# Agent attention and maxout layer on one core: a side path's transfers on GpSimd's queue, 72 transfers instead of 74, agents loaded as 28 partitions

## The chip, the cores and the metric

The kernel runs on one core of a Trainium2 chip. The metric is device time in microseconds (us), the median of several runs. Two kernels that differ by less than about 0.2% cannot be told apart by it. One execution was also recorded by the hardware profiler; the span of its page runs from the first to the last instruction.

## The reference

With B = 4, N = 12544, C = 128, 49 agent rows per batch and d_ff = 768:

```python
sm = softmax(scale * a @ b.T)
agent_v = sm(agents, k) @ v            # [4, 49, 128]
x = (sm(q, agents) @ agent_v)          # [4, 12544, 128]
h = max(x @ w1, x @ w2, x @ w3)        # [50176, 768]
out = h @ w_out                        # [50176, 128], float32
```

q, k and v are float32 and 25.7 MB each; the output is as large.

## The kernel before

The keys are worked in 56 groups of seven tiles of 128 rows (operations `kc`, `kt`, `ke`, `ks`, `kx`, `vc`, `kv`), the queries in 49 groups of eight tiles (`qc` to `ov`); group 48 takes the two tiles left over of each batch. Each output row is a mixture of the 49 rows of `agent_v`, and the kernel folds the maxout layer into small tables `G` per batch, so that a query group needs few products. That folding has room for CAPACITY = 64 hidden units that are undecided; whether the room is enough is computed on the chip (`c0`, `c1`, `good`, `worst`), read into a register on every engine (line 274), and tested by a branch (line 275). When the test fails, `in_general` (lines 635 to 737) computes everything again without the folding. With the given inputs the test holds and the branch skips it.

The graph of operations is built in `graph`, and the string ORDER lists all of them in the order in which they are emitted; each engine runs its own in that order. Operands wait in numbered slots (`SLOTS`): LD has five slots for loaded float32 groups, OS five for outputs, QT three for transposed queries.

All the large transfers are issued by SyncE (SP), in ORDER's order: 32 loads of k and v (`kl`, `vl`, line 302), four weights (line 349), 17 loads of q (`ql`, line 553) and 20 stores (`st`, line 561). A store waits for the scaling operations `ov` (line 628 on VectorE; for the second half of group 47 line 631 on ScalarE) that fill its part of an OS slot. Stores up to group 44 take three query groups, 24 tiles, 12 KB per partition. The last groups go alone: 45 and 46 as eight tiles each, 47 in two halves of four tiles, and 48, whose store stands ahead of group 44's.

The agents are the one transfer outside SP in the part that runs: ScalarE's queue issues it first of all (line 217), as 49 partitions of four rows, one row per batch, into the tile `sums_of`. `prep` (lines 287 to 296) casts them to bf16, transposes them batch by batch on TensorE, and copies each of the four results to `agT`, which the scores of the keys need.

The landing of each transfer is told by a semaphore. There are eight of these for the transfers of SP and ScalarE together, taken in turn in the order of the program, so the ninth transfer uses the first one's again. The skipped path's own transfers (lines 652, 668, 704, 737) are on ScalarE's queue in this kernel, and so belong to the same eight. Because the skipped path would have moved these semaphores, an engine that skips it has to bring them to the values that the path would have left: these are the semaphore instructions that the profile puts at line 275. The instructions at line 870 end the program: SP waits for all semaphores, two in an instruction, the transfers' eight in their order, and then the engines meet.

Of the kernel before, what the change touches and what calls it, by code (L numbers as in the profile page):

```python
# [24 lines left out]
VC = C + 2  # L25
CAPACITY = 64
LEAST, MOST = 1e-15, 1e15
KEYS, EARLY = B * A, WHOLE * 3 + 6
TG, TK = 3, 4
LONG = TG * GT  # L30

PE, ACT, DVE, POOL, SP = range(5)
# [77 lines left out]
def graph(plan, em):  # L110
# [52 lines left out]
    for s in range(NQ):  # L163
        parts = parts_of(s)
        np_ = len(parts)
        gx, gy = [f"gx{p[0]}" for p in parts], [f"gy{p[0]}" for p in parts]
        z = s // TG * TG
        if s == z:
            add(f"ql.{s}", SP, em.q_load(s), new=[("LD", f"q.{s}")], **dma(524 if s == NQ - 1 else TG * 524))
        add(f"qc.{s}", POOL, em.q_cast(s), (0.98, 1.1), after=[f"ql.{z}"], new=[("QB", f"qb.{s}")], use=[f"q.{z}"])  # L170
        add(f"qt.{s}", PE, em.q_turn(s), mm(GT, 128), after=[f"qc.{s}", "prep"], new=[("M", f"qT_ps.{s}")], use=[f"qb.{s}"])
        add(f"qe.{s}", ACT, em.q_evacuate(s), act(1024), after=[f"qt.{s}"], new=[("QT", f"qT.{s}")], use=[f"qT_ps.{s}"])
        add(f"sc.{s}", PE, em.q_scores(s), mm(2 * np_, 512 // np_), after=[f"qe.{s}"], new=[("M", f"qs.{s}")], use=[f"qT.{s}"])
        add(f"ex.{s}", ACT, em.q_exps(s), (0.478, 0.655), after=[f"sc.{s}"], new=[("EQ", f"e.{s}")], use=[f"qs.{s}"])
        add(f"su.{s}", PE, em.sums(s), mm(GT // 2, 2), after=[f"ex.{s}"], use=[f"e.{s}", f"qs.{s}"])
        add(f"re.{s}", DVE, em.recips(s), (0.118, 0.3), after=[f"su.{s}"], use=[f"qs.{s}"])
        add(f"u.{s}", PE, em.hidden(s, GU, "u"), mm(np_, 512 // np_), after=[f"ex.{s}"] + gx, new=[("M", f"u.{s}")], use=[f"e.{s}"])
        add(f"a.{s}", ACT, em.relu_first(s), act(512), after=[f"u.{s}"], new=[("AS", f"a.{s}")], use=[f"u.{s}"])
        add(f"v.{s}", PE, em.hidden(s, GV, "v"), mm(np_, 512 // np_), after=[f"ex.{s}"] + gx, new=[("M", f"v.{s}")], use=[f"e.{s}"])
        add(f"x.{s}", DVE, em.max_second(s), dve(512), after=[f"v.{s}", f"a.{s}"], new=[("R", f"r.{s}")], use=[f"v.{s}", f"a.{s}"])  # L180
        add(f"p.{s}", PE, em.out_products(s), (0.9, 1.1), after=[f"x.{s}", f"ex.{s}"] + gy, new=[("M", f"o.{s}.{h}") for h in range(2)],
            use=[f"e.{s}", f"r.{s}"])
        for h in range(2):
            eng = ACT if h and s == NQ - 2 else DVE
            add(f"ov.{s}.{h}", eng, em.out_scale(s, h, eng), (0.7, 0.9) if eng == ACT else (0.6, 0.72), after=[f"p.{s}", f"re.{s}"],
                new=[("OS", f"os.{s}")] if h == 0 and s == z else [],
                use=[f"o.{s}.{h}"] + ([] if h == 0 and s == z else [f"os.{z}"]))
        alone = s >= NQ - 1 - TG
        if s == NQ - 2:
            for h in range(2):  # L190
                add(f"st.{s}.{h}", SP, em.store(s, h), after=[f"ov.{s}.{h}"], use=[f"os.{z}"], cost=(0.45, 1.6), serve=262 / 415.0)
        elif alone or s == z + TG - 1:
            add(f"st.{s}", SP, em.store(s), after=[f"ov.{i}.{o}" for i in ([s] if alone else range(z, z + TG)) for o in range(2)],
                use=[f"os.{z}"], cost=(0.45, 1.6), serve=(524 if alone else TG * 524) / 415.0)
    add("c0", POOL, em.in_range(0), (3.0, 3.2), after=[f"re.{s}" for s in range(EARLY)] + [f"nr{b}" for b in range(B)])
# [5 lines left out]
class Emit:  # L201
    def __init__(self, tc, pools, io):
# [12 lines left out]
        self.sums_of = const.tile([P, KEYS + NQ * GT], FP32, name="sums_of")  # L215
        self.ag_st = self.sums_of[:A, :B * C].rearrange("a (b c) -> a b c", b=B)
        nc.scalar.dma_start(self.ag_st, io["agents"].rearrange("b a c -> a b c"))
        self.fold = const.tile([P, A], FP32, name="fold")
# [4 lines left out]
        for v in self.slots["VB"]:  # L223
            nc.vector.memset(v[:, :, C:], 1.0)
        self.ag_bf = const.tile([A, B, C], BF16, name="ag_bf")
        self.agT = const.tile([P, B, H], BF16, name="agT")
# [60 lines left out]
    def prep(self):  # L287
        nc = self.nc
        nc.vector.tensor_copy(out=self.ag_bf, in_=self.ag_st)
        t, u = self.psum[:, 0, :].bitcast(BF16), self.psum[:, 1, :]  # L290
        for b in range(B):
            nc.tensor.transpose(t[:, b * H:b * H + A], self.ag_bf[:, b, :], self.ident[:A, :A])
        self.mul(u[:, :H], self.ones, self.earlier[:, 1:1 + H], True)
        for b in range(B):
            nc.vector.tensor_copy(out=self.agT[:, b, :A], in_=t[:, b * H:b * H + A])
        nc.vector.tensor_copy(out=self.slot_of, in_=u[:, :H])
# [239 lines left out]
    def far(self, name, s, n):  # L536
# [7 lines left out]
        rows = flat[row:row + LONG * P, :].rearrange("(p j) c -> p j c", j=LONG)  # L544
        return rows if n == LONG else rows[:, s % TG * GT:(s % TG + 1) * GT, :]

    def near(self, s, tile_, n):
        if s == NQ - 1:
            return tile_[:, :GT, :].rearrange("p (b j) c -> p b j c", j=2)
        return tile_[:, :LONG, :] if n == LONG else tile_[:, s % TG * GT:(s % TG + 1) * GT, :]  # L550

    def q_load(self, s):
        return lambda: self.nc.sync.dma_start(self.near(s, self.t[f"q.{s}"], LONG), self.far("q", s, LONG))

    def store(self, s, h=None):
        def fn():
            n = LONG if s < NQ - 1 - TG else GT
            far, near = self.far("out", s, n), self.near(s, self.t[f"os.{s // TG * TG}"], n)
            if h is not None:
                far, near = (x[:, 4 * h:4 * h + 4, :] for x in (far, near))  # L560
            self.nc.sync.dma_start(far, near)
        return fn

# [75 lines left out]
    def keys_in_general(self):  # L639
# [11 lines left out]
        def scores(b, g):  # L651
            nc.scalar.dma_start(kf[:, :KT, :], rows("k", b, g))
            nc.gpsimd.tensor_copy(out=kb, in_=kf[:, :KT, :])
# [5 lines left out]
        for b in range(B):  # L659
# [6 lines left out]
            for g in range(NCH):  # L666
                scores(b, g)
                nc.scalar.dma_start(vf[:, :KT, :], rows("v", b, g))
                nc.gpsimd.tensor_copy(out=vb, in_=vf[:, :KT, :])
# [14 lines left out]
    def queries_in_general(self):  # L684
# [13 lines left out]
        for s in range(NQ):  # L698
# [4 lines left out]
            of = [p[0] for p in parts for _ in range(p[4])]  # L703
            nc.scalar.dma_start(self.near(s, q, GT), self.far("q", s, GT))
            nc.gpsimd.tensor_copy(out=qb, in_=q[:, half, :])
# [21 lines left out]
            for o in range(2):  # L727
# [3 lines left out]
                for f in range(NF):  # L731
                    for j in range(4):
# [3 lines left out]
                                        in1=rc[:, 4 * o:4 * o + 4].unsqueeze(2).to_broadcast([P, 4, C]), op=ALU.mult)  # L736
            nc.scalar.dma_start(self.far("out", s, GT), self.near(s, out, GT))

# [103 lines left out]
qe.47/0 su.46 u.46/0 ov.44.1 v.46/3 a.46/2 re.46 sc.47/6 st.44 x.45/1 ex.47/0 x.46/2 p.45/7,5 su.47 p.46/1,2 ov.45.0/1 u.47/0  # L842
re.47 v.47/4 ov.45.1 a.47/0 ov.46.0 st.45 ov.46.1 x.47/0 c1 st.46 p.47/3,7 good ov.47.1 ov.47.0 st.47.0 st.47.1 worst
"""
# [30 lines left out]
```

## Time and profile before

| | us |
|---|---|
| median of three runs | 255.36 |
| the three runs | 255.23 to 255.63 |
| the profiled execution, its time | 255.66 |
| the profiled execution, its span | 253.7 |

Busy shares of the span: PE 81%, DVE 66%, POOL 60%, ACT 58%. 104.91 MB moved at a mean of 414 GB/s. The profiled execution took 1.96 us more than its span, and lies 0.30 us above the median. Lines at which no engine is busy, such as 275 and 870, are read from the view of one source line, which gives count, durations, and the start of the first and the last instruction of each kind.

### The profile page before, as it was taken

Reading aid. Unit: us, or ns where it says so; the run is one execution under the profiler, and the core shown is the slowest. Engines: PE = TensorE matmul, PEld = TensorE weight load, DVE = VectorE, ACT = ScalarE, POOL = GpSimd, SP = SyncE. Lnnn points to the kernel's source line nnn. Section 1 sums busy time; section 2 is a strip of 40 time slices with the busy share of each in tenths; the row PEclk is TensorE's granted clock in tenths of the full one; section 3 lists DMA queues with packets and bytes.
Section 4 is the critical chain, followed back from the end, with each engine's and each line's share of the span. In section 5 each row is a group of like instructions: output and inputs, shape, how many; then the busy total and the mean of one; then the engine's idle time right before and its main releaser. Section 6 shows DMA issues by size and latency. Waiting matters only on the chain.

```text
span 253.7 us, 6350 instructions
## 1 busy us (share of the span) xinstructions
PE 205.3 (81%) x2484; PEld 149.1 (59%) x2506; DVE 167.9 (66%) x360; ACT 147.2 (58%) x240; POOL 151.1 (60%) x171
## 2 busy tenths in 40 slices
PE   0694687759999979998999689998988989999710
PEld 0472654738686657776767466765666665676400
DVE  6442612684686689675766976494848999888920
ACT  2346267217585758285757584666566887776510
POOL 2251742796979386979690699686664443449000
PEclk9999568698999999999999999999999999999975
DMA  6999999999999999999999999999999999999992
GB/s 258 439 432 420 428 432 424 429 427 430 426 419 420 430 428 433 422 431 421 430 422 440 422 433 420 431 426 416 432 430 424 426 421 424 429 426 427 415 398 104
DMA packets 11520, 104.91 MB, mean 414 GB/s; under 512 B 1175, under 2 KB 2395, under 8 KB 4443
## 3 DMA queue, kind: packets, MB, share of 16 engines
q1 hardware_dynamic: 11280, 104.34, 97.5%
q8 instruction: 21, 0.34, 0.5%
q10 hardware_dynamic: 203, 0.10, 0.1%
q14 instruction: 16, 0.13, 0.1%
HBM read 78.74 MB, written 25.69 MB: 412 GB/s over the span
## 4 chain that ended last, share of the span: by engine, by line
PE 61%; DVE 13%; ACT 9%; DMA 7%; issue 4%; POOL 1%; ACTq 0%; DVEq 0%; POOLq 0%
PE psum L285 45%; PE psum L317 16%; DMA LD<-in_k_dram 5%; ACT QT L577 4%; DVE OS L628 3%; DMA sums_of<-in_agents_dram 2%; ACT EQ L589 2%; DVE KT L323 2%; ACT VB L310 1%; DVE gap L435 1%; DVE R L612 1%; ACT EK L334 1%; POOL KB L312 1%; ACT AS L609 1%; DVE open L438 1%
## 5 line engine op out<-in xcount | busy, mean ns | idle before, releaser
L312 POOL CAST KB<-LD 128x896 bf16<-128x896 f32 x56 | 52.6, 972 | 43.9 <-DMA LD<-in_k_dram 27.6
L571 POOL CAST QB<-LD 128x1024 bf16<-128x1024 f32 x49 | 49.8, 1046 | 26.1 <-DMA LD<-in_q_dram 17.7
L628 DVE TENSOR_TENSOR OS<-psum,sums_of 128x512 f32<-128x512 f32 x97 | 61.1, 678 | 4.7 <-PE psum L285 4.5
L577 ACT ACTIVATE QT<-psum 128x1024 bf16<-128x1024 bf16 x49 | 50.2, 1025 | 18.5 <-PE psum L317 17.8
L323 DVE COPY KT<-psum 128x896 bf16<-128x896 bf16 x56 | 34.3, 620 | 25.2 <-PE psum L317 21.3
L285 PE MATMUL psum<-VB,EK 128*128 128x260 bf16 x224 | 40.0, 281 | 4.5 <-ACT VB L310 2.6
L334 ACT ACTIVATE EK<-psum 128x343 bf16<-128x343 f32 x56 | 25.6, 466 | 24.8 <-PE psum L285 15.3
L609 ACT ACTIVATE AS<-psum 128x512 bf16<-128x512 f32 x49 | 29.0, 597 | 17.9 <-PE psum L285 15.9
L612 DVE TENSOR_TENSOR R<-psum,AS 128x512 bf16<-128x512 f32 x49 | 32.7, 679 | 9.4 <-PE psum L285 4.3
L312 POOL CAST VB<-LD 128x896 bf16<-128x896 f32 x42 | 38.5, 957 | 0.3 <-DMA LD<-in_v_dram 0.3
L317 PE MATMUL psum<-ident,KB 128*128 128x128 bf16 x392 | 35.2, 240 | 4.1 <-POOL KB L312 3.2
L589 ACT ACTIVATE EQ<-psum 128x512 bf16<-128x512 f32 x49 | 29.3, 597 | 13.4 <-PE psum L285 12.6
L285 PEld LDWEIGHTS <-EK 128*128 128x128 bf16 x224 | 20.5, 103 | 24.1 <-issue 16.7
L317 PEld LDWEIGHTS <-KB 128*128 128x128 bf16 x392 | 27.5, 108 | 8.1 <-POOL KB L312 3.8
L285 PEld LDWEIGHTS <-EQ 128*128 128x128 bf16 x392 | 25.9, 97 | 10.6 <-ACT EQ L589 5.7
L317 PE MATMUL psum<-ident,QB 128*128 128x128 bf16 x392 | 30.6, 222 | 0.1
L285 PE MATMUL psum<-G,R 128*128 128x256 bf16 x196 | 29.4, 273 | 1.3 <-DVE R L612 1.2
L285 PE MATMUL psum<-G,EQ 128*128 128x256 bf16 x196 | 29.4, 272 | 0.2
L317 PEld LDWEIGHTS <-QB 128*128 128x128 bf16 x392 | 23.4, 99 | 7.3 <-issue 5.7
L285 PE MATMUL psum<-EQ,G 128*128 128x512 bf16 (+1 forms) x82 | 24.5, 363 | 0.9 <-DVE sums_of L599 0.4
L285 PE MATMUL psum<-QT,agT 128*64 128x512 bf16 (+1 forms) x104 | 20.1, 384 | 6.2 <-ACT QT L577 6.2
L285 PE MATMUL psum<-agT,KT 128*128 128x49 bf16 x392 | 20.7, 191 | 2.9 <-DVE KT L323 2.7
(97 smaller groups left out, 178.2 us busy)
## 6 DMA issues: line engine op xcount, KB each, us to landing
LD<-in_q_dram SPq DMA_DIRECT2D x16, 1536.0 KB, 16.8
out_dram<-OS SPq DMA_DIRECT2D x15, 1536.0 KB, 20.2
LD<-in_k_dram SPq DMA_DIRECT2D x12, 1792.0 KB, 14.8
LD<-in_v_dram SPq DMA_DIRECT2D x12, 1792.0 KB, 15.7
LD<-in_k_dram SPq DMA_DIRECT2D x4, 896.0 KB, 14.7
LD<-in_v_dram SPq DMA_DIRECT2D x4, 896.0 KB, 13.4
out_dram<-OS SPq DMA_DIRECT2D x3, 512.0 KB, 10.0
LD<-in_moe_w_dram SPq DMA_DIRECT2D x3, 384.0 KB, 13.3
```

The costliest lines, as they stand in the source:

```text
L285: self.nc.tensor.matmul(out, w, x, start=start, stop=True, skip_group_check=True)
L310: self.nc.scalar.activation(out, src, AF.Copy)
L312: self.nc.gpsimd.tensor_copy(out=out, in_=src)
L317: self.nc.tensor.transpose(t[:, j * P:(j + 1) * P], src[:, j, :], self.ident)
L323: return lambda: self.nc.vector.tensor_copy(out=self.t[f"kT{r}"], in_=self.t[f"kT_ps{r}"].bitcast(BF16)[:, :KT * C])
L334: self.nc.scalar.activation(e[:, :, :A], s, AF.Exp, scale=SCALE)
L571: return lambda: self.nc.gpsimd.tensor_copy(out=self.t[f"qb.{s}"], in_=self.half("q", s))
L577: return lambda: self.nc.scalar.activation(self.t[f"qT.{s}"].rearrange("p j c -> p (j c)"), self.t[f"qT_ps.{s}"].bitcast(BF16), AF.Copy)
L589: return lambda: self.nc.scalar.activation(self.t[f"e.{s}"], self.t[f"qs.{s}"], AF.Exp, scale=SCALE)
L609: return lambda: self.nc.scalar.activation(self.t[f"a.{s}"], self.t[f"u.{s}"], AF.Relu)
L612: return lambda: self.nc.vector.tensor_tensor(out=self.t[f"r.{s}"], in0=self.t[f"v.{s}"], in1=self.t[f"a.{s}"], op=ALU.max)
L628: self.nc.vector.tensor_tensor(out=out, in0=src, in1=rc.unsqueeze(2).to_broadcast([P, 4, C]), op=ALU.mult)
```

## The change

Three things are changed.

1. In the skipped path the four kinds of transfer are issued by GpSimd (`nc.gpsimd.dma_start`) rather than by ScalarE.
2. The last stores are cut otherwise. A table `STORES` gives for each group that ends a store how many groups it takes: three up to group 44, then group 46 stores 45 and 46 together (16 tiles), and 47 and 48 go whole (8 tiles). In ORDER `st.45` goes, and `st.47.0 st.47.1` becomes `st.47`. That makes 18 stores and 72 transfers with the agents.
3. The agents are loaded as 28 partitions of seven consecutive rows, 3584 B each, into a part of the last OS slot, and cast into a part of the last QT slot. `prep` makes seven transposes of 28 rows instead of four of 49, each into 28 of 32 columns, and one copy with a four-dimensional pattern instead of four copies. Row 49b + 7q' + j of the list is row j of partition 7b + q'.

```diff
+STORES = {**{s: TG for s in range(TG - 1, NQ - 1 - TG, TG)}, NQ - 3: 2, NQ - 2: 1, NQ - 1: 1}
...
-        alone = s >= NQ - 1 - TG
-        if s == NQ - 2:
-            for h in range(2):
-                add(f"st.{s}.{h}", SP, em.store(s, h), after=[f"ov.{s}.{h}"], use=[f"os.{z}"], cost=(0.45, 1.6), serve=262 / 415.0)
-        elif alone or s == z + TG - 1:
-            add(f"st.{s}", SP, em.store(s), after=[f"ov.{i}.{o}" for i in ([s] if alone else range(z, z + TG)) for o in range(2)],
-                use=[f"os.{z}"], cost=(0.45, 1.6), serve=(524 if alone else TG * 524) / 415.0)
+        if s in STORES:
+            n = STORES[s]
+            add(f"st.{s}", SP, em.store(s, n), after=[f"ov.{i}.{o}" for i in range(s - n + 1, s + 1) for o in range(2)],
+                use=[f"os.{z}"], cost=(0.45, 1.6), serve=n * 524 / 415.0)
...
-        self.ag_st = self.sums_of[:A, :B * C].rearrange("a (b c) -> a b c", b=B)
-        nc.scalar.dma_start(self.ag_st, io["agents"].rearrange("b a c -> a b c"))
+        self.ag_st, self.ag_bf = self.slots["OS"][-1][:AP_, :A // 7, :], self.slots["QT"][-1][:AP_, :A // 7, :]
+        nc.scalar.dma_start(self.ag_st, io["agents"].rearrange("b a c -> (b a) c").rearrange("(p j) c -> p j c", p=AP_))
...
-        for b in range(B):
-            nc.tensor.transpose(t[:, b * H:b * H + A], self.ag_bf[:, b, :], self.ident[:A, :A])
+        t = t[:, :A // 7 * 32].rearrange("c (j x) -> c j x", x=32)[:, :, :AP_]
+        for j in range(A // 7):
+            nc.tensor.transpose(t[:, j, :], self.ag_bf[:, j, :], self.ident[:AP_, :AP_])
...
-        for b in range(B):
-            nc.vector.tensor_copy(out=self.agT[:, b, :A], in_=t[:, b * H:b * H + A])
+        nc.vector.tensor_copy(out=self.agT[:, :, :A].rearrange("c b (q j) -> c j b q", j=A // 7), in_=t.rearrange("c j (b q) -> c j b q", b=B))
...
-            nc.scalar.dma_start(kf[:, :KT, :], rows("k", b, g))
+            nc.gpsimd.dma_start(kf[:, :KT, :], rows("k", b, g))
...
-                nc.scalar.dma_start(vf[:, :KT, :], rows("v", b, g))
+                nc.gpsimd.dma_start(vf[:, :KT, :], rows("v", b, g))
...
-            nc.scalar.dma_start(self.near(s, q, GT), self.far("q", s, GT))
+            nc.gpsimd.dma_start(self.near(s, q, GT), self.far("q", s, GT))
...
-            nc.scalar.dma_start(self.far("out", s, GT), self.near(s, out, GT))
+            nc.gpsimd.dma_start(self.far("out", s, GT), self.near(s, out, GT))
...
-re.47 v.47/4 ov.45.1 a.47/0 ov.46.0 st.45 ov.46.1 x.47/0 c1 st.46 p.47/3,7 good ov.47.1 ov.47.0 st.47.0 st.47.1 worst
+re.47 v.47/4 ov.45.1 a.47/0 ov.46.0 ov.46.1 x.47/0 c1 st.46 p.47/3,7 good ov.47.1 ov.47.0 st.47 worst
```

More of the change, by code (lines that the diff above doesn't have):

```diff
@@ L544, in far @@
         rows = flat[row:row + LONG * P, :].rearrange("(p j) c -> p j c", j=LONG)
-        return rows if n == LONG else rows[:, s % TG * GT:(s % TG + 1) * GT, :]
+        return rows if n == LONG else rows[:, (s % TG + 1) * GT - n:(s % TG + 1) * GT, :]
     def near(self, s, tile_, n):
@@ L549, in near, with store @@
             return tile_[:, :GT, :].rearrange("p (b j) c -> p b j c", j=2)
-        return tile_[:, :LONG, :] if n == LONG else tile_[:, s % TG * GT:(s % TG + 1) * GT, :]
+        return tile_[:, :LONG, :] if n == LONG else tile_[:, (s % TG + 1) * GT - n:(s % TG + 1) * GT, :]
     def q_load(self, s):
         return lambda: self.nc.sync.dma_start(self.near(s, self.t[f"q.{s}"], LONG), self.far("q", s, LONG))
[L555 to L562, printed above, removed]
+    def store(self, s, n):
+        return lambda: self.nc.sync.dma_start(self.far("out", s, n * GT), self.near(s, self.t[f"os.{s // TG * TG}"], n * GT))
     def rc(self, s):
```

3 lines of the change are left out of this document (1 added, 2 removed).

## The prediction, made before the changed kernel was run

> **What bounds the kernel now.** I read the page first, for which resource is full; then the stretches of the last ten microseconds; then the instructions at the two lines that end the program. From the page:
>
> ```profile
> span 253.7 us, 6350 instructions
> ...
> PE 205.3 (81%) x2484; PEld 149.1 (59%) x2506; DVE 167.9 (66%) x360; ACT 147.2 (58%) x240; POOL 151.1 (60%) x171
> ...
> DMA  6999999999999999999999999999999999999992
> GB/s 258 439 432 420 428 432 424 429 427 430 426 419 420 430 428 433 422 431 421 430 422 440 422 433 420 431 426 416 432 430 424 426 421 424 429 426 427 415 398 104
> ...
> q1 hardware_dynamic: 11280, 104.34, 97.5%
> ```
>
> No compute engine is near its span, while the 16 DMA engines are busy in tenths of 9 from the second slice to the last but one. SP's queue q1 alone fills 97.5% of them. The time is bytes over DMA rate, plus a start, plus an end. The same bytes are moved after the change, so only start, end and evenness can give anything. The end, by stretches (start:end, length, busy time of the five engines, TensorE clock, share of the DMA engines, GB/s):
>
> ```profile
> 244.00:245.00 1.00, 0.00 (x0) 0.00 (x0) 0.00 (x0) 0.00 (x0) 0.00 (x0) 0.50 1.02 426
> 245.00:246.00 1.00, 0.00 (x0) 0.00 (x0) 0.00 (x0) 0.00 (x0) 0.00 (x0) 0.50 0.94 383
> 246.00:247.00 1.00, 0.00 (x0) 0.00 (x0) 0.00 (x0) 0.00 (x0) 0.00 (x0) 0.50 0.81 328
> ...
> 248.00:249.00 1.00, 0.00 (x0) 0.00 (x0) 0.00 (x0) 0.00 (x0) 0.00 (x0) 0.50 0.63 242
> 249.00:250.00 1.00, 0.00 (x0) 0.00 (x0) 0.00 (x0) 0.00 (x0) 0.00 (x0) 0.50 0.40 148
> ...
> 251.50:253.70 2.20, 0.00 (x0) 0.00 (x0) 0.00 (x0) 0.00 (x0) 0.00 (x0) 0.50 0.00 0
> ```
>
> All five engines are idle for ten microseconds, in two parts. First the DMA engines run dry one after another: the share falls from 1.02 at 244 to 0.40 at 249. They do not hold equal work, and the one that holds most sets the end. Then 2.2 us pass in which nothing moves. What fills these stands in the views of lines 561 (issues after 243), 275 (SP, after 251.5) and 870: count, duration in ns, first and last start.
>
> ```profile
> L561 SPq DMA_DIRECT2D out_dram<-OS x1: 619/619/619, 243.0 to 243.0; - x1
> ...
> DMA to landing us min/median/max: 8.8/8.8/8.8
> ```
>
> ```profile
> L275 SPq EVENT_SEMAPHORE  x7: 17/17/17, 251.8 to 252.3; - x7
> ```
>
> ```profile
> L870 SPq EVENT_SEMAPHORE  x10: 17/28/28, 252.3 to 253.6; - x10
> ...
> L870 SPq DRAIN  x3: 7/7/7, 252.8 to 253.2; - x3
> ```
>
> The last store is issued at 243.0 and landed at 251.8. From there SP runs in single file: seven semaphore instructions of line 275 to 252.3, eight of line 870 to 252.8, then the engines' meeting to 253.7. That is 0.5 + 0.5 + 0.9 = 1.9 us, about 0.07 us an instruction, all behind the last byte. The chain of waits on the page instead ends in engines' work, since it follows the last busy instruction; it says nothing of these ten microseconds.
>
> **The change part by part.** *The skipped path's queue.* None of it runs. What runs is the bookkeeping of the skip. SP's instructions at line 275 wait for each of the eight landing semaphores in turn (the row above has the seven behind the last landing), because the skipped path would use the same ones. With its transfers on GpSimd's queue they get semaphores of their own, SP has nothing to make up, and the seven behind the last landing go: -0.5. If the program still makes SP do it, 0. POOL must make up its own eight instead: 8 x 0.07 = 0.6 us from 249.4 (row below), done by 250.1, under the cover of the transfers that end at 251.8. Without this cover it would cost 0.6. Line 870 may grow by eight semaphores, two in an instruction: 4 x 0.07 = 0.3 if they stand behind the last store's, 0 if ahead of it. I take 0: SP reaches them before the landing.
>
> *72 transfers.* The views of the issues count them:
>
> ```profile
> LD<-in_q_dram SPq DMA_DIRECT2D x16, 1536.0 KB, 16.8
> out_dram<-OS SPq DMA_DIRECT2D x15, 1536.0 KB, 20.2
> LD<-in_k_dram SPq DMA_DIRECT2D x12, 1792.0 KB, 14.8
> LD<-in_v_dram SPq DMA_DIRECT2D x12, 1792.0 KB, 15.7
> LD<-in_k_dram SPq DMA_DIRECT2D x4, 896.0 KB, 14.7
> LD<-in_v_dram SPq DMA_DIRECT2D x4, 896.0 KB, 13.4
> out_dram<-OS SPq DMA_DIRECT2D x3, 512.0 KB, 10.0
> LD<-in_moe_w_dram SPq DMA_DIRECT2D x3, 384.0 KB, 13.3
> LD<-in_q_dram SPq DMA_DIRECT2D x1, 512.0 KB, 21.3
> out_dram<-OS SPq DMA_DIRECT2D x2, 256.0 KB, 8.8
> ```
>
> These 72, one load of `w_out` and the agents are 74. Over eight semaphores in turn, the 74th sits on the second, so after its landing seven of line 870's eight waits still have to be run; the 72nd sits on the eighth, and the other seven are behind SP when it lands. 7/8 of 0.5 is 0.45: -0.45. If line 870 takes them in another order, 0.
>
> *The merged stores.* `st.46` now waits for both its groups and is issued when the old `st.46` was; half of its bytes come 1.2 us later than the old `st.45`:
>
> ```profile
> 239.35 0.33 SPq L561 DMA_DIRECT2D out_dram<-OS  x1
> ```
>
> ```profile
> 240.55 0.33 SPq L561 DMA_DIRECT2D out_dram<-OS  x1
> ```
>
> Behind the waiting `st.46` on SP stands only `st.47`, whose data come at 243.0 either way, when the old second half was issued. A store of that size is 10.0 us from issue to landing, so the engine that ends last holds over 8 us of older work at 240.55: 1.2 us are hidden, 0. Without this backlog it would be +1.2. Per DMA engine 32 data packets become 16, and two end packets go. A packet's fixed part: 196 agent packets of 512 B take 28 ns each (next row), at 26.1 B/ns (7.14 MB in 100.6% of 16 x 17 us) 19.6 of it are bytes, so 8 ns; 18 x 8 = 0.15. I take -0.1, between 0 and -0.15.
>
> ```profile
> q1 hardware_dynamic: 1167, 7.14, 100.6%
> ```
>
> *The agents.* The window 1.6 to 5.7, in which they load (queue q10), and the window 20 to 22, which holds one fetch of instructions:
>
> ```profile
> q10 hardware_dynamic: 203, 0.10, 8.4%
> ```
>
> ```profile
> q8 instruction: 1, 0.02, 2.8%
> ```
>
> 203 packets are 196 rows and seven end packets: the 49 partitions lie on seven DMA engines, seven on each. 8.4% of 16 x 4.1 us is 5.5 us, 0.79 on each of the seven and none on the other nine. After the change a packet is 3584 B, 0.14 us at 26.1 B/ns, 28 in all. If 28 partitions go to fourteen engines, each carries two, 0.27; if to seven, four, 0.55. The engine that ends last sets the end. If it is one of the seven it gains 0.79 - 0.27 = 0.52; if not, it gains nothing or loses 0.27. That engine carries extra work by the falling shares above, and the agents' is known to lie on seven alone, so I count it among them. Some of it may be hidden in the start, before the first loads flow; I take -0.4, between +0.27 and -0.79.
>
> The Trainium skill, page "DMA: Bandwidth & Descriptors", section "Why a DMA increments its semaphore by 16 and not by 1", says that a transfer is spread over the largest number of engines up to 16 that divides its slowest dimension, and on SP's and ScalarE's queues over the lowest-numbered ones; by that 49 gives seven, as the seven end packets show, and 28 gives fourteen, with 0.27 added on engines eight to fourteen. By this rule alone the agents' term would be -0.52.
>
> *`prep`.* Before:
>
> ```profile
> 6.25 1.04 DVE L289 CAST ag_bf<-sums_of 49x512 bf16<-49x512 f32 x1 [0.83 <-DMA sums_of<-in_agents_dram]
> ...
> 7.73 0.46 DVE L295 COPY agT<-psum 128x49 bf16<-128x49 bf16 x4 [0.44 <-PE psum L292]
> ...
> 11.69 0.33 SPq L302 DMA_DIRECT2D LD<-in_k_dram  x1
> ```
>
> The cast ends its wait up to 0.83 sooner, but has 896 columns: at 1.04 x 896/512 that is 1.82, 0.78 longer, at worst. Seven transposes instead of four lie between the two rows' 7.29 and 7.73, at most 0.33 more. One copy replaces four; I bound it by 0 and 0.46. So `agT` comes between 1.3 us sooner (a cast no longer than now) and 1.1 later (no earlier landing). The first transfer that hangs on it is the one at 11.69, and the DMA engines are at 9 tenths all through the second to the fifth slice: 0. Without that cover it would be these -1.3 to +1.1.
>
> **The sum.** -0.5 - 0.45 - 0.1 - 0.4 = -1.45. Against the profiled execution's own 255.66 (span 253.7 and 1.96 around it) that is 254.2. This execution lies 0.30 above the median of 255.36, so for a median I say 255.36 - 1.45 = **253.9**.
>
> **The rivals.**
>
> *Half of it.* Either the line 275 work stays on SP, or line 870's order is otherwise, or the last engine is not among the agents' seven. Against: seven instructions each stand visibly behind the landing. For: nothing in the trace shows where the program would put the new semaphores. One of the two 0.5s not gained gives 254.4; both gained and the agents at 0 gives 254.3; one not gained and the agents at 0 gives 254.8. Around 254.6.
>
> *Nothing.* The extra work on the last engine is not the agents' but instruction fetches. One fetch takes 2.8% of 16 x 2 us, 0.9 us, on a single DMA engine. `prep` has six more TensorE instructions and the skipped path other code, which may move fetches. One more on the last engine costs 0.9, and takes the agents' gain and one of the 0.5s away: 255.36 - 1.45 + 0.9 = 254.8; with the line 275 work also left on SP, 255.3, no change. This is also the case in which the edit does not do what it says.
>
> *Slower: POOL's way out of the branch.* From the view of line 275:
>
> ```profile
> L275 POOLq COMPARE_BRANCH  x1: 45/45/45, 243.5 to 243.5; - x1
> ...
> L275 POOLq EVENT_SEMAPHORE  x1: 17/17/17, 249.4 to 249.4; - x1
> ```
>
> POOL takes the branch at 243.5 and runs its next instruction at 249.4: 5.9 us for the code behind the branch to come through busy DMA engines. It then needs one instruction; after the change nine or so. If these run over the end of the fetched block, a second fetch follows, up to 5.9 again: 249.4 + 0.6 + 5.9 = 255.9, and with SP's last wait for POOL and the engines' meeting, 0.9, a span of 256.8: +3.1 on 253.7, a median of 258.5. It decides from the point where POOL is done after 252.8, when SP comes to its drain in before, that is with a second fetch of over 2.8 us. Against: a handful of instructions rarely meets a block's end, and the DMA engines are nearly free by 250, so a second fetch would be shorter.
>
> The Trainium skill, page "Runtime: NRT & Kernel Launch", section "Instruction fetch mechanics", says that a taken branch out of the fetched window must fetch its target through a DMA before going on. The 5.9 us agree; a second fetch no run here shows yet.
>
> **How the numbers follow.** The forecast, 253.9: 0.58; half, around 254.6: 0.20; nothing, around 255.2: 0.14; slower: 0.08. The range has as its low end the best bounds, -0.5 - 0.45 - 0.15 - 0.79 = -1.9, with 0.1 for the runs' spread of 255.23 to 255.63: 253.3. Its high end takes in the half case with 0.1 above 254.8: 254.9. That leaves out the last two cases, 0.22. A measurement of this kernel tells 0.2%, 0.51 us, from no change, so faster means below 254.85: the first case and nearly all of the second, and a little of the third, 0.79. Same 0.13, slower 0.08.
>
> **What would show each step.** Line 275 on SP: no semaphore instructions behind the last landing; if eight stand there still, the first term falls. Line 870: one instruction between the last landing and SP's drain; if seven or more, the second falls. POOL: eight or so more instructions at line 275, ending before the last landing. Agents: q10 with some 42 packets (28 and fourteen end packets), a landing well before 6.2, and the last transfer's landing 0.4 to 0.5 earlier than 251.8. Stores: the last one landing under 10 us from its issue, and the DMA share at 1.0 through 245 as before. The prediction is wrong if the last landing stays at 251.8 or the stretch from it to the end stays near 1.9.

## The result, and the profile after

| | before | after |
|---|---|---|
| median of 22 runs each, us | 255.61 | 254.15 |
| the profiled execution, time / span, us | 255.66 / 253.7 | 254.07 / 252.2 |
| last landing, us from the span's start | 251.83 | 251.23 |
| from the last landing to the end, us | 1.82 | 0.95 |

The ratio of the runs, each set beside its neighbours, is 0.9955, with a 95% interval of 0.9941 to 0.9968. On 255.4 that is 1.15 us faster, 0.8 to 1.5. The medians in the table differ by 1.46; the means without the three slow runs, 255.47 and 254.32, differ by 1.16, as the ratio has it, and the ratio is what the text goes by. The forecast was 1.45 less, 253.9 in a range of 253.3 to 254.9. The landings in the table are from the records of the sixteen parts of the last transfer, one for each DMA engine.

The page of the changed kernel: the span, the DMA engines' busy tenths and GB/s in 40 slices, three queues, and the last stores.

```profile
span 252.2 us, 6372 instructions
...
DMA  6999999999999999999999999999999999999994
GB/s 252 437 425 427 431 428 429 429 422 430 429 422 427 426 433 426 427 425 428 421 431 434 422 434 421 429 430 419 431 426 427 425 424 424 428 424 424 429 417 169
...
q1 hardware_dynamic: 10992, 104.34, 97.9%
q8 instruction: 21, 0.34, 0.5%
q10 hardware_dynamic: 42, 0.10, 0.2%
...
out_dram<-OS SPq DMA_DIRECT2D x2, 512.0 KB, 11.1
```

The middle is as before: 9 tenths from the second slice on, and q1 moves the same 104.34 MB, now in 288 packets fewer (11280 - 10992), 18 on each of the 16 engines. What changed shows at the end. The last ten microseconds, by stretches:

```profile
244.00:245.00 1.00, 0.00 (x0) 0.00 (x0) 0.00 (x0) 0.00 (x0) 0.00 (x0) 0.50 0.97 414
245.00:246.00 1.00, 0.00 (x0) 0.00 (x0) 0.00 (x0) 0.00 (x0) 0.00 (x0) 0.50 0.99 414
246.00:247.00 1.00, 0.00 (x0) 0.00 (x0) 0.00 (x0) 0.00 (x0) 0.00 (x0) 0.50 0.75 315
...
249.00:250.00 1.00, 0.00 (x0) 0.00 (x0) 0.00 (x0) 0.00 (x0) 0.00 (x0) 0.50 0.38 147
250.00:251.00 1.00, 0.00 (x0) 0.00 (x0) 0.00 (x0) 0.00 (x0) 0.00 (x0) 0.50 0.18 61
```

The DMA engines still run dry one after another: the sixteen landings of the last store spread over 5.1 us, against 5.8 before. What went is the stretch behind them. The view of the line of the branch (now 272), GpSimd and SP:

```profile
L272 POOLq EVENT_SEMAPHORE  x5: 17/43/43, 248.1 to 248.5; - x5
L272 POOLq COMPARE_BRANCH  x1: 45/45/45, 243.5 to 243.5; - x1
L272 SPq COMPARE_BRANCH  x1: 50/50/50, 244.0 to 244.0; - x1
L272 POOLq INC_SWDGE_SEM  x1: 177/177/177, 248.6 to 248.6; - x1
```

SP has no semaphore instruction left there. The view of the line that ends the program (now 861), SP from the last landing on:

```profile
L861 SPq EVENT_SEMAPHORE  x3: 17/17/28, 251.2 to 252.1; - x3
L861 SPq DRAIN  x3: 7/7/7, 251.3 to 251.6; - x3
```

One semaphore instruction stands between the landing at 251.2 and the first drain at 251.3; the two others belong to the engines' meeting.

### The profile page after: what moved, and what is told of

The parts are those of the page before. It is cut to its first block, busy times and chain, and to the rows that moved or that the text cites. A ratio compares the mean times of both kernels' runs of the same rounds, so it can differ in the third digit from the quotient of the medians.

```text
span 252.2 us, 6372 instructions
## 1 busy us (share of the span) xinstructions
PE 207.6 (82%) x2509; PEld 149.2 (59%) x2509; DVE 167.8 (67%) x357; ACT 147.3 (58%) x240; POOL 151.1 (60%) x171
## 3 DMA queue, kind: packets, MB, share of 16 engines
q1 hardware_dynamic: 10992, 104.34, 97.9%
## 4 chain that ended last, share of the span: by engine, by line
PE 62%; DVE 15%; ACT 10%; DMA 5%; issue 4%; POOL 1%; ACTq 0%; DVEq 0%; POOLq 0%
PE psum L282 46%; PE psum L314 15%; DMA LD<-in_k_dram 5%; ACT QT L568 4%; DVE OS L619 3%; ACT EQ L580 2%; DVE KT L320 2%; ACT VB L307 1%; DVE gap L432 1%; DVE R L603 1%; ACT EK L331 1%; POOL KB L309 1%; DVE cand L431 1%; ACT AS L600 1%; DVE open L435 1%
## 5 line engine op out<-in xcount | busy, mean ns | idle before, releaser
L282 PE MATMUL psum<-EQ,G 128*128 128x512 bf16 (+1 forms) x104 | 31.3, 366 | 0.4 <-DVE OS L619 0.2
```

Source lines behind the costliest of these rows:

```text
L282: self.nc.tensor.matmul(out, w, x, start=start, stop=True, skip_group_check=True)
```

## The experiments

Each row is one kernel; the ratio is to the kernel before, run beside it on the same chip. "Last landing" and "behind it" are those of the one profiled execution.

| | median, us (runs) | ratio [95%] | last landing | behind it |
|---|---|---|---|---|
| before | 255.61 (22) | | 251.83 | 1.82 |
| after | 254.15 (22) | 0.9955 [0.9941, 0.9968] | 251.23 | 0.95 |
| e1_queue | 254.7 (12) | 0.998 [0.9967, 0.9993] | 251.32 | 1.31 |
| e2_stores | 254.96 (12) | 0.9992 [0.9981, 1.0004] | 251.21 | 1.39 |
| e3_agents | 255.1 (12) | 0.9994 [0.9982, 1.0006] | 251.11 | 1.82 |
| e7_no_agents | 254.66 (12) | 0.9983 [0.997, 0.9995] | 251.33 | 0.97 |
| after_again | 254.33 (12) | 0.9974 [0.9958, 0.999] | 251.17 | 0.95 |
| e8_no_branch | 253.49 (6) | 0.9927 [0.991, 0.9945] | 250.72 | 0.87 |
| e11_no_branch_again | 253.62 (6) | 0.9943 [0.9923, 0.9963] | 250.77 | 0.87 |
| e10_old_agents_no_branch | 253.54 (6) | 0.9936 [0.9914, 0.9957] | 251.36 | 0.87 |
| e9_mid | 256.54 (10) | 1.0049 [1.0034, 1.0064] | 253.24 | 1.45 |
| e4_more | 260.15 (1) | | 256.96 | 1.31 |
| e6_mid | 258.77 (1) | | 255.66 | 1.31 |
| e5_probe | 261.4 (1) | | | |

**The three parts, each alone on the kernel before.** First the queue of the skipped path:

```diff
-            nc.scalar.dma_start(kf[:, :KT, :], rows("k", b, g))
+            nc.gpsimd.dma_start(kf[:, :KT, :], rows("k", b, g))
...
-            nc.scalar.dma_start(self.far("out", s, GT), self.near(s, out, GT))
+            nc.gpsimd.dma_start(self.far("out", s, GT), self.near(s, out, GT))
```

> The kernel before with the skipped path's four transfers on GpSimd's queue and nothing else (74 transfers, agents and stores as before). Theory: the last landing stays at 251.8 (within 0.3), SP has no semaphore instruction left at the branch's line, some seven of the program's last line still follow the landing, so landing to end falls from 1.8 to about 1.35 and the time by 0.5 (ratio 0.998). Rival 1, the edit does nothing because none of it runs: landing to end 1.8, ratio 1.000. Rival 2, the gain was all the drain's order by this edit: landing to end 0.95, ratio 0.9965.

The end of the program in this kernel, SP from the last landing at 251.3 on:

```profile
L870 SPq EVENT_SEMAPHORE  x9: 17/28/28, 251.3 to 252.6; - x9
L870 SPq DRAIN  x3: 7/7/7, 251.8 to 252.1; - x3
```

Nine semaphore instructions, of which two belong to the meeting: seven are left, for there are 74 transfers still. The first drain comes 0.5 after the landing. Behind the landing 1.82 became 1.31, 0.52 less by the unrounded ends of 1.825 and 1.309: the seven of line 275, as forecast. The last landing was expected to stay within 0.3 of 251.8 and came at 251.32; why is said under *The level* below.

Then the cut of the stores alone, with 72 transfers and the skipped path on ScalarE's queue:

```diff
+STORES = {**{s: TG for s in range(TG - 1, NQ - 1 - TG, TG)}, NQ - 3: 2, NQ - 2: 1, NQ - 1: 1}
...
-re.47 v.47/4 ov.45.1 a.47/0 ov.46.0 st.45 ov.46.1 x.47/0 c1 st.46 p.47/3,7 good ov.47.1 ov.47.0 st.47.0 st.47.1 worst
+re.47 v.47/4 ov.45.1 a.47/0 ov.46.0 ov.46.1 x.47/0 c1 st.46 p.47/3,7 good ov.47.1 ov.47.0 st.47 worst
```

> The kernel before with the new stores alone (72 transfers; skipped path on ScalarE's queue, agents as before). Theory: SP still runs its eight semaphore instructions at the branch, but the last store sits on the eighth, so they are behind it and only the program's last line (eight, then the meeting) follows: landing to end about 1.4 instead of 1.8, last landing 251.7 (0.1 sooner by fewer packets), time 0.5 to 0.6 lower (ratio 0.998). Rival, the larger packets of the merged stores give the gain: the last landing falls by 0.4 or more and landing to end stays 1.8. Rival, the merge costs: last landing later than 252.1.

The line of the branch (273 here), all of SP, and after it the end (line 862) from the last landing on:

```profile
L273 SPq EVENT_SEMAPHORE  x8: 17/17/17, 244.0 to 251.2; - x8
```

```profile
L862 SPq EVENT_SEMAPHORE  x10: 17/28/28, 251.3 to 252.5; - x10
L862 SPq DRAIN  x3: 7/7/7, 251.8 to 252.1; - x3
```

The eight waits at the branch's line are still there, but now only the eighth is behind the landing; in the kernel before they ran from 251.2 to 252.3. So the number of transfers decides how many of *them* are late, while the eight at the end of the program stand behind in full. Behind the landing 0.44 went (1.825 to 1.389). The forecast had put this term at the end of the program. That is where it falls once the queue is changed as well: only with both edits does one instruction remain. The sum, 0.88 by the after kernel's 0.947, is near the forecast's 0.95. In time the runs of this kernel show less than the 0.5 to 0.6 expected: 0.9992 is 0.2 us, and the interval includes no change at all. The price of this part is thus read from the profile, not from the times.

Then the agents alone:

```diff
-        nc.scalar.dma_start(self.ag_st, io["agents"].rearrange("b a c -> a b c"))
+        nc.scalar.dma_start(self.ag_st, io["agents"].rearrange("b a c -> (b a) c").rearrange("(p j) c -> p j c", p=AP_))
```

> The kernel before with the agents as 28 partitions of seven rows and the prep that goes with it, nothing else. Theory: the engine that ends last was one of the seven that carried the agents, so the last landing comes 0.4 to 0.5 sooner (251.35) and landing to end stays 1.8; ratio 0.998. Rival, it is not among them: last landing 251.8 or later, ratio 1.000 to 1.001. Rival, an earlier agT is what helps (compute was on the path): the first load that waits for compute comes sooner and every later landing with it by 0.7, ratio 0.997.

Behind the landing nothing moved (1.82). The ratio is 0.9994, 0.15 us, with an interval that includes no change at all. The last landing, 251.11, is as early as the theory asked, but e1_queue and e2_stores land at 251.2 to 251.3 with the agents' old form, so it is no sign of the agents. The third possibility, a ratio of 0.997 by an earlier `agT`, falls. The three ratios together are 0.0034 under one, 0.87 us; the whole change was measured at 1.15, and at 0.66 in a second series (below).

**Two loads more, at the start.** To double what the agents cost, two further loads of the old form were put behind the agents' own:

```diff
+        for i in range(2):
+            nc.scalar.dma_start(self.slots["OS"][i][:A, :B, :], io["agents"].rearrange("b a c -> a b c"))
```

> The changed kernel with the agents loaded twice more in the old form (49 partitions of four rows, two loads into unused parts of two OS slots), 74 transfers. It computes the same. Each such load puts 0.66 to 0.79 us on the seven lowest engines. Theory: the engine that ends last is among the seven, so the last landing moves from 251.2 by 2 x 0.66 to 2 x 0.79, to 252.5 to 252.8; and since the last store sits on the second of the eight semaphores again, landing to end rises from 0.95 to about 1.35. Rival, the last engine is another one: the last landing stays at 251.2 to 251.5 until one of the seven overtakes it.

As a measure of the load this run is spoiled. Each added load takes one of the eight landing semaphores, so SP's early loads had to wait until these came free: the load of weights issued at 11.33 in the changed kernel goes out at 17.78, the next load of v at 26.26 instead of 15.84. The page shows the hole in the fourth and fifth slice.

```profile
GB/s 240 429 422 276 285 432 435 422 431 423 426 428 408 434 423 426 431 425 433 416 426 442 420 431 428 422 432 425 423 426 431 428 419 428 429 428 421 422 417 138
```

Of its 6 us none can be put down to the seven engines. What it does show is the count: with 74 transfers again, 1.31 us stand behind the last landing.

**Probes.** Six tiny loads behind the last store, over 8, 4, 2, 1, 12 and 14 partitions, were meant to tell which DMA engine is the last.

```diff
+PROBES = (8, 4, 2, 1, 12, 14)
...
+    def probe(self, n):
+        return lambda: self.nc.sync.dma_start(self.slots["LD"][3][:n, 0, :], self.io["q"][0, :n, :])
```

> The changed kernel with six loads of 512 B rows behind the last store, on 8, 4, 2, 1, 12 and 14 partitions; what they load is used for nothing. A load of so many partitions ends on so many DMA engines, so its landings tell which of the sixteen landings of the last store belong to the lowest engines. Theory: the landings that come late (three microseconds and more after the first) belong to fixed engines; the last one is among the lowest seven, and the load of 8 partitions lands 0.1 to 0.2 after the last store. Rival: the last engine is a high one, and the load of 8 lands ahead of the last store's end by 0.3 or more. The time is 0.3 to 0.6 above the changed kernel's, since 78 transfers end on the sixth semaphore and three instructions follow.

The probes write the same rows and so waited for one another, which made the time 261.4 instead of the 0.3 to 0.6 more that was expected; only the first, of eight partitions, is of use. Its eight landings (246.75 to 251.47) come behind eight of the last store's, seven of them by some 0.2 us. The latest is at 251.47, ahead of the store's own last landing at 251.72. In this one execution the engine that ended last was therefore not one of the probe's eight. Whether these eight hold the agents' seven no record shows.

**Two loads more, in mid-run,** at some 39 us, where no early load waits for their semaphores; first run once, then ten times (the same kernel):

```diff
+    for i in range(2):
+        add(f"ax.{i}", SP, em.more(i), cost=(0.45, 1.6), serve=0.2)
...
+    def more(self, i):
+        return lambda: self.nc.sync.dma_start(self.slots["OS"][3][:A, i * B:(i + 1) * B, :], self.io["agents"].rearrange("b a c -> a b c"))
```

> The changed kernel with two loads of the agents in the old form (49 partitions of four rows) on SP's queue in the middle of the run, at some 45 us, into an unused part of an OS slot; they are used for nothing. 74 transfers. Theory: the engine that ends last is among the seven, so the last landing moves by 2 x 0.66 to 2 x 0.79, from 251.2 to 252.5 to 252.8, and the spread of the last transfer's sixteen landings from 5.1 to 6.4 or more; landing to end 1.3. Rival: another engine ends last, the last landing moves by 0.5 or less.

This single run is inconclusive: its GB/s are low in slices 2 to 4 (380, 363, 406 against 437, 425, 427), before the added loads start.

> The changed kernel with two further loads of the agents in the old form (49 partitions of four rows of 512 B, 392 packets on seven DMA engines, some 1.6 us of packets on each of the seven) in mid-run at some 41 us, 74 transfers in all. The stretch behind the last landing is 1.31 us for 74 transfers (+0.36 on the changed kernel's 0.95). Theory (the DMA engine with the most work sets the end, wherever in the run the work is added): last landing +1.0 to +1.4 on 251.2, spread of the last store's sixteen landings 6.2 us or more against 5.1, median 255.5 to 255.9. Rival (an added load of one engine is evened out before the end, by slots and queues): last landing +0.5 at most, spread 5.1, median 254.5 to 255.0.

In the ten runs' profile (e9_mid) these slices are as in the changed kernel. The window 50 to 60, queue q1 of the changed kernel, and of this one:

```profile
q1 hardware_dynamic: 342, 4.23, 99.7%
```

```profile
q1 hardware_dynamic: 699, 3.87, 101.1%
```

The queue is just as full and moves 0.36 MB less. The 392 added packets of 512 B took 13.86 us by their records, 1.98 on each of seven engines, more than the 1.6 of the expectation. The q load issued at 48 us lands at 65.60 where it landed at 63.05, and the delay of some two microseconds is never made up: the last landing is at 253.24, 2.01 later. That is more than the theory's 1.0 to 1.4, and the median, 256.54, lies above its 255.5 to 255.9. Its other mark failed: the sixteen landings of the last store spread over 3.0 us, not 6.2. So it was not one lagging engine at the end. The stretches tell what happened:

```profile
240.00:241.00 1.00, 0.75 (x10) 0.30 (x8) 0.98 (x4) 0.99 (x2) 0.00 (x0) 1.00 0.81 335
...
245.00:246.00 1.00, 0.15 (x2) 0.14 (x3) 0.96 (x4) 0.00 (x0) 0.00 (x0) 1.00 0.73 307
246.00:247.00 1.00, 0.62 (x5) 0.27 (x3) 0.97 (x5) 0.50 (x2) 0.00 (x0) 1.00 0.96 406
247.00:248.00 1.00, 0.00 (x0) 0.00 (x0) 0.48 (x3) 0.64 (x3) 0.00 (x0) 1.00 1.01 418
```

The last groups are computed some five microseconds later than in the changed kernel, DVE is busy throughout, and the DMA share drops to 0.73 while the last store waits (it is issued at 247.7, not 242.8). Loads came late, so the work did, and so the stores. The issues of the next two loads on SP also took 4.9 and 4.2 us rather than 0.33; how much of the delay is theirs this run can't tell, though the DMA share stays near 1.0 meanwhile. It is therefore no clean price for the agents' bytes. Behind the landing 1.45 stand, 0.14 more than the 1.31 that the count of 74 gives in e1_queue, e4_more and e6_mid. The trace has the reason: of SP's waits at the program's end one stood for 172 ns instead of 28, until VectorE came out of the branch at 253.6.

```profile
L866 SPq EVENT_SEMAPHORE  x9: 17/28/172, 253.3 to 254.6; - x9
```

```profile
L274 DVEq EVENT_SEMAPHORE  x1: 21/21/21, 253.6 to 253.6; - x1
```

**The agents against the same kernel, beside it.** The changed kernel with the agents' old form, and the changed kernel again, in one series:

```diff
-CAPACITY, AP_ = 64, B * 7
+CAPACITY = 64
...
-        for j in range(A // 7):
-            nc.tensor.transpose(t[:, j, :], self.ag_bf[:, j, :], self.ident[:AP_, :AP_])
+        for b in range(B):
+            nc.tensor.transpose(t[:, b * H:b * H + A], self.ag_bf[:, b, :], self.ident[:A, :A])
```

> The changed kernel with the agents as before (49 partitions of four rows, four transposes, four copies): queue and stores alone. Theory: against the changed kernel of the same call 0.15 to 0.45 us slower (ratio to the kernel before 0.9965 to 0.9975), landing to end 0.95 as in the changed kernel, all of the difference in the last landing. Rival: the agents' load gives nothing, the same time as the changed kernel within 0.1 us.

> The changed kernel once more, beside the one above. Ratio to the kernel before 0.9955, landing to end 0.95, last landing 251.0 to 251.4: how far the last landing moves between two profiles of one kernel is what this is for.

0.9983 against 0.9974: the new form is worth 0.23 us here. That lies in the theory's 0.15 to 0.45, but the two intervals overlap so far that no gain, the rival, is not excluded. This series gave less for the whole change than the 22 runs did, 0.9974 against 0.9955; the intervals overlap.

**Without the branch.** What the DMA engines carry besides the stores in the last microseconds is code. The window 245 to 251 of the changed kernel:

```profile
q1 hardware_dynamic: 259, 1.35, 55.4%
q8 instruction: 2, 0.03, 2.6%
q14 instruction: 6, 0.05, 2.4%
```

Eight fetches, 5% of 16 x 6 us, 4.8 us of DMA engine time, for the engines' way out of the branch. They are taken away with the branch:

```diff
-        with self.tc.If(worst > CAPACITY):
-            self.in_general()
```

> The changed kernel without the branch and the path behind it (the fallback of 64 undecided units is left out; it does not run with these inputs). In the changed kernel the last landing is at 251.2 us, and the sixteen landings of its last store end at 251.23 with the second last at 250.82; the last engine has a jump of some 1.4 us around 246 us, when the code behind the branch is fetched. Theory (what sets the last engine at the end is the fetches behind the branch): no fetches at 247 us, the last landing at 250.8 (0.4 earlier), the landing-to-end stretch 0.95 or shorter, a median 0.3 to 0.6 us under the changed kernel's 254.15, so 253.5 to 253.9. Rival (the last engine is set by the fetches of the straight code, and the one behind the branch falls on any engine): the last landing at 251.2 within 0.15, a median within 0.2 of 254.15 unless the stretch behind the landing shrinks.

The same window has no fetch left:

```profile
q1 hardware_dynamic: 265, 1.38, 55.2%
```

The last landing came at 250.72 (250.8 expected), and 0.87 stood behind it rather than 0.95, with a median of 253.49, 0.66 below the changed kernel's (253.5 to 253.9 expected). The rival, a landing within 0.15 of 251.2, falls. This kernel can't stand in for the others, since it has no fallback; it shows what it costs to branch past a path that does not run.

This gave a theory for the agents: the fetches make some other engine the last, and hide what the agents' engines gain. If so, the gain should appear without the branch. The old form (the edit of e7_no_agents) and the new, both without the branch, side by side:

> The changed kernel without the branch and the path behind it (left out: the fallback of 64 undecided units), and with the agents loaded and prepared in the old form of 49 partitions on seven DMA engines. To be set against the same kernel with the new form, run beside it. With the branch in place the agents' new form was worth 0.15 us (-0.46 to +0.15) and some 0.23 us rather than the 0.4 forecast. Theory (the fetches behind the branch make another engine the last, and so cap the agents' gain): without the branch the new form is worth 0.4 or more: this kernel 253.9 or more, 0.4 to 0.6 above its partner, last landing 251.1 or later. Rival (the new form's packets are slow at the start, so that its engines carry 0.3 to 0.6 us rather than the 0.27 forecast, or the extra work of the start is hidden there): 0.1 to 0.3 above its partner as before, about 253.7, last landing 250.8 to 251.0.

> The changed kernel without the branch and the path behind it once more, as the partner of the run with the agents' old form. It had 253.49 us, last landing 250.72, 0.87 us from there to the end. If that was no accident: 253.3 to 253.8, last landing 250.6 to 250.9, 0.87 behind it. If the 0.5 us by which its last landing was earlier was chance: a last landing of 251.1 to 251.3 and 254.0 or more.

The second run repeats: 253.62, last landing 250.77. But the old form is no slower: 253.54. The theory asked for 0.4 to 0.6, the rival for 0.1 to 0.3, and the difference is -0.08. The ranges, 253.22 to 254.02 and 253.43 to 253.85, leave no room for the theory's 0.4. The fetches do not hide a gain of that size. (The profiled execution of the old form, with its landing at 251.36, is the slowest of its six, 254.02; in it the last store is issued at 245.7, late as in e9_mid, against 242.4 in e8_no_branch and 244.4 in e11_no_branch_again. By itself it says nothing of the agents.)

## Why the prediction was right, and where it was not

*What bounds the kernel.* Right: the middle did not move, and what the profiles show as gained lies at the end. Some 0.18 us more was gained outside the profile's span, where the prediction had no term (*The level*, below).

*The skipped path's queue, -0.5.* Right, in mechanism and size: e1_queue has 0.52 less behind the last landing, and its whole ratio of 0.998 is 0.51 us (0.18 to 0.84). That these two agree so closely is partly chance, since some 0.18 of the time was gained outside the span. SP has nothing at the branch's line. The four further instructions that SP got at the program's end (14 rather than 10) run between 248.7 and the landing, as was taken.

*72 transfers, -0.45.* Right in size: 0.44 alone, and 0.36 on top of the queue (1.309 to 0.947). The place was right for the two edits together; alone it works through line 275. The times of e2_stores alone, 0.2 us, do not show this term by themselves.

*Merged stores, -0.1.* The cover held. `st.46` is issued at 240.33, and the last store as follows, with its time from issue to landing:

```profile
L553 SPq DMA_DIRECT2D out_dram<-OS x1: 333/333/333, 242.8 to 242.8; - x1
...
DMA to landing us min/median/max: 8.5/8.5/8.5
```

It landed 8.5 us after its issue, under the 10 named as the mark, and the DMA share stood at 0.97 and 0.99 through 246. The 18 packets fewer per engine are there; the 0.1 itself is too small to be told apart by any run here.

*GpSimd's way out: slower.* It fell. The next instruction ran 4.6 us behind the branch (243.5 to 248.1), it took six rather than nine, and all were done at 248.8, 2.4 before the last landing. No second fetch stood between them. The Trainium skill, page "Runtime: NRT & Kernel Launch", section "Instruction fetch mechanics", has a taken branch fetch its target before it goes on when the target lies outside the fetched window; the rows agree, and e8_no_branch shows besides that such fetches cost the transfers beside them some 0.45 us of last landing. The rival of one more fetch on the last engine did not come either: both kernels have 21 fetches on queue q8 and 16 on q14.

*The agents, -0.4.* **This is the term that was mis-sized.** Three comparisons give -0.15 (alone on before), -0.23 (both forms with the branch) and +0.08 (both without), a mean of -0.1, and none of them can be told from nothing. What the step named did occur. The window in which the agents load, 1.6 to 5.7:

```profile
q10 hardware_dynamic: 42, 0.10, 12.0%
```

42 packets are 28 and fourteen end packets, so the fourteen engines are as the Trainium skill's rule gives them (page "DMA: Bandwidth & Descriptors", section "Why a DMA increments its semaphore by 16 and not by 1"). But their time was wrong: 12.0% of 16 x 4.1 us is 7.9 us, 0.56 on each of fourteen, not 0.27. The median packet did take 0.14 us; the longest took 0.8. In other executions the sum was 4.6 us (e3_agents) to 9.4 (e9_mid), so 0.33 to 0.67 an engine, against 0.79 before: 0.12 to 0.46 were there to be gained on seven engines, and seven others got 0.33 to 0.67 more.

What came of it stands in the landing records of the next transfers. The load of weights that SP issues at some 7 us lands on its sixteen engines one by one. In the five profiled executions with the old form (before, e1_queue, e2_stores, e7_no_agents, e10_old_agents_no_branch) the first of the sixteen landings comes at 17.49 on average and the last at 18.46 (18.22 to 18.69); in six with the new form (after, e3_agents, after_again, e8_no_branch, e11_no_branch_again, e9_mid) at 17.80 and 18.40 (18.18 to 18.56). So the new form did make the engines more even, but by holding back those that were ahead. The engine that was last gained 0.06 us. The step that failed is thus the gain of the last engine, 0.79 - 0.27 = 0.52, taken as -0.4: the runs show 0.06 there and 0.1 in the times.

The choice of that engine fits the execution that it was read from. In before, nine engines land this load 0 to 0.54 us behind the first, and seven 0.68 to 1.21, as the seven with the agents would. The one at 1.21 can be followed to the end by its landings, which from 24 us on lie 0.66 or more behind all others. But it falls back by some 1.6, 1.6 and 1.4 us more, each time in the stretch in which a fetch of queue q8 runs, the first, ninth and seventeenth of the 21 (at 20.9, 116.6 and 208.9 us). These 4.5 us of the 5.78 by which it is the last at the end fall together with fetches of code and not with the agents. In the changed kernel the engine that is last up to the store before the last two (4.68 behind the first) is overtaken: one that was 3.2 to 3.3 behind falls back by 1.8 to 2.0 us in the stretch of the branch's fetches and ends last, 0.41 behind the next. Whether the 0.06 is all that ever reaches the end can't be told from these runs; no larger gain is shown.

*`prep`.* Right, nothing at the end. The start of the changed kernel, in order of time:

```profile
5.46 0.61 DVE L286 CAST QT<-OS 28x896 bf16<-28x896 f32 x1
...
6.53 0.91 DVE L292 COPY agT<-psum 128x196 bf16<-128x196 bf16 x1 [0.45 <-PE psum L290]
...
10.95 0.33 SPq L299 DMA_DIRECT2D LD<-in_k_dram  x1
```

The cast waits for no transfer any more and is shorter than before (0.61 against 1.04), not longer, with 28 partitions instead of 49 and 1.75 times the columns. In before, GpSimd's first cast runs beside it all the time (from 6.08); here that begins at 5.88 and meets only its last 0.2 us. Which of the two shortened it was not separated. `agT` is ready at 7.44 instead of 8.19, and the load that hangs on it is issued 0.74 sooner, at 10.95. In e3_agents the same happens, and the time is within 0.15 us of before: the full DMA queues hide it.

*The level.* The profiled execution of before was a late one: its last landing, 251.83, is 0.5 later than in e1_queue, e2_stores and e7_no_agents, all at 251.2 to 251.3. So of the 0.60 by which the landing moved between the two profiles, most is that one execution's. The 0.88 behind the landing are firmer: the same ends stand in a second profile of each kind (1.824 in e3_agents beside 1.825, 0.946 in after_again beside 0.947).

A second part lies outside the span, and no term of the prediction holds it. Each run has a time and a span. The time is the longer one by 2.02 us on average in the kernel before (28 runs beside e1_queue, 1.95 to 2.11), by 2.04 in e2_stores and 2.01 in e3_agents, but by 1.84 in e1_queue (11 runs, 1.76 to 1.90), 1.84 in the changed kernel and 1.83 in e7_no_agents and after_again. So moving the skipped path to GpSimd's queue also took some 0.18 us off the time, outside the profile's span; why stays open.

0.88 and 0.18 make 1.06 of the 1.15. The 0.1 left can't be told from nothing, and in the second series the whole was 0.66 (0.26 to 1.07), which leaves nothing over. So the total came as near as it did partly by luck: the 0.5 forecast for agents and packets did not show, and 0.18 that was not forecast did. The range also held the case of both waits gained and the agents at 0, 254.3, so the measured 254.15 does not by itself speak for the sum of 253.9.

## What to carry to other kernels

Look at what stands behind the last landing: waits that run in single file on the issuing engine cost 0.06 to 0.07 us each, and their number follows from which semaphore the last transfer got and from which queues a path uses that is not even taken. That part can be counted in the rows, and the count held to within 0.1 us, except where another engine came out of the branch later than the landing (0.14 in e9_mid). A few tenths on some DMA engines at the start can't be forecast so. Spreading the work more evenly gains only what the latest engine has less to do, and the landings of each transfer show which that is and when it fell back.

## What the runs showed of the hardware beside this

- A branch that is taken past code costs even where every engine idles. Without it the last landing was 0.45 us earlier (250.72 and 250.77 against 251.23 and 251.17), since eight fetches no longer shared the DMA engines with the last stores.
- A delay of mid-run was not made up in e9_mid: after 392 packets of 512 B (1.98 us on each of seven engines) at 53 to 57 us, a load landed 2.5 us later at 65.6, and the last landing of all was still 2.01 us later at 253.24. SP's two issues of 4.9 and 4.2 us may have a part in it.
- A fetch of code on a busy DMA engine set that engine back by more than its own record: in before, three fetches of q8 with records of 0.88 to 0.91 us stand beside 1.4 to 1.6 us of later landings on one engine, eight fetches apart.
- The time outside the profile's span was 2.0 us in the kernels whose skipped path is on ScalarE's queue and 1.84 with GpSimd's.
- The cast of 28 x 896 elements took 0.61 us, that of 49 x 512 took 1.04, the latter with a cast of GpSimd beside it from start to end.
